# Start-up loads, warm-up, one scaling and the raw weight loads moved in a single-core fp32 transformer block

## The chip, the core and the metric

The kernel runs on one NeuronCore of a Trainium2 chip. The time is the device time in microseconds (us) of one execution; the median of several runs is compared. Engines are named as in the profile: PE (TensorE, matmul), PEld (its weight load), DVE (VectorE), ACT (ScalarE), POOL (GpSimd), SP (SyncE, which here only issues DMAs).

## The reference

One adaLN transformer block: 2048 tokens, width 640, 32 heads of 20, MLP width 1728, all in fp32.

```python
mod = (_silu(c) @ w_mod).reshape(c.shape[0], 6, 1, -1)
sa, ca, ga, sb, cb, gb = (mod[:, 0], mod[:, 1], mod[:, 2], mod[:, 3], mod[:, 4], mod[:, 5])
h = _layernorm(x, axis=-1) * (1 + ca) + sa
x = x + ga * _A_ref(h, A_wqkv, A_w_phi, A_wo)
h = _layernorm(x, axis=-1) * (1 + cb) + sb
x = x + gb * _B_ref(h, B_w1, B_b1, B_w2, B_b2)
```

`_A_ref` is linear attention: q and k are multiplied per head by `w_phi`, turned into features by two softmaxes (of the value and of its negative), and O = phi_q (phi_k^T V) / (phi_q phi_k^T 1), followed by `wo`. `_B_ref` is an MLP whose activation is the square of relu: `r = relu(x @ w1 + b1)`, then `(r * r) @ w2 + b2`.

## The kernel before

**Arithmetic.** Every fp32 operand of a large product is split into a high part and a low part in a reduced format: ACT writes the high part (an activation with Copy, or with the real function), DVE then the low part (`lo`, line 80). A product is the sum of three PE passes, high by high, high by low, low by high (`three` and `mm`, line 70). So each weight tile needs a "hi" on ACT and a "lo" on DVE before PE may use it, and it occupies a slot of the pool `w` (21 slots of 128 x 2 x 640).

**Stages** (times of the profiled execution). The start, to about 60 us: a hand-written order for all five engines (`first`, a manual schedule that begins on line 180). The middle, 60 to 245 us: q, k and v of the other token tiles, laid out by a scheduler. Then the attention numerators, `wo` and the second layer norm, 245 to 350 us. Then the MLP in four groups of 512 tokens (`group(g)`, g = 0 to 3), with a piece of attention between the second and the third. In the groups PE, DVE and ACT follow the code (`by_hand`), SP and POOL are ordered by the scheduler.

**The start in detail.** SP loads, in order: c_t, the transposed conditioning vector (128 x 5, line 183); bd_t, `w_phi` as a block-diagonal matrix (128 x 640, line 185); the raw k weights (`load_raw`, a piece of 40 rows on line 190, five of 128 x 640 on line 192); the first pair of token tiles xb; the raw q weights; the modulation weights wm and so on. Completion semaphores of DMAs are handed out in rotation, eight of them, so the ninth load is issued when the first has landed.

PE begins with `WARM` matmuls on a tile of ones (line 553; each is two passes in the profile, so 28 for 14), then folds: `fold(nm, d)` multiplies one chunk of the raw weight by bd_t (line 241; 12 passes) into two PSUM tiles of the tag `pj`, which has four buffers, so two folds fill it. `split` writes the high parts on ACT (line 248) and the low parts on DVE (line 80), and these free the buffers. ACT's own order in the start is: table load and the exponential ce of c_t (line 222, for silu(c)), neg (line 227), then the splits of the folds. The folds of k come first, then the statistics and scaling of the first tile pair (`stats`, line 486; `scale`, line 502: two activations on line 504), the folds of q, and the modulation vectors cols_a.

Then `k_step(d)`, d = 0 to 4, accumulates chunk d of the k product pk of two token tiles. It needs chunk d of the transposed, modulated input: ACT's hfa (line 338) and hT (line 340) and DVE's low half (line 80), which `out0(d + 1)` issues one step ahead. In that loop the statistics of the second tile pair XB[1] are taken after d = 1 and its scaling issued after d = 2:

```python
        if d == 1:
            n1 = stats(XB[1], "a1")
        if d == 2:
            scale(XB[1], *n1)
```

After the loop ACT makes one high part of the v weights (`v_hi`, line 595) and takes pk out of PSUM (`to_sb`, k on line 391); pq uses the same four buffers next.

**The MLP weights.** 28 pieces (W1 and W2, 14 chunks each, the last one half wide), each loaded raw (rw, line 1065 for W1, 1067 for W2), then split (hi on line 1074, lo on line 80). `prep_load` takes the next slot from a list `places` and loads the raw piece into a row of the pools s1, s2 or s4; `prep_hi` and `prep_lo` fill the slot. Slots are used in rotation, so a new piece takes one that another tile has held, among these XM[j], the residual rows of token tile pair j. `group(0)` issues the loads, splits and lows a few pieces ahead of PE: `p_load(2 * f + 11 - ...)` makes sure that 2f + 11 of the pieces are issued by step f.

**Second layer norm in the groups.** `back(j)` stores the normalised rows of pair j to memory (xn, on ACT's queue, line 1150) and loads them back block by block (sb, four DMAs on SP, line 1161); `turn(j)` transposes them on DVE (fa_q, lines 1171 and 1172). `up` products (matmul with W1) go to ACT for bias and relu (r, line 1375) and for the square (r2t, lines 1384 and 1387), `acc` and `acr` are the products with W2.

## Time and profile before

| what | value |
| --- | --- |
| three runs | 788.79, 790.90, 790.81 us; median 790.81 |
| the profiled execution | 790.26 us |
| its span in the trace | 788.6 us (so 1.66 us lie around the span) |
| PE busy | 777.0 us, 99% of the span |
| DVE, ACT, POOL busy | 553.8, 403.0, 76.5 us |
| DMA | 142.31 MB, mean 180 GB/s |

Rows of the profile give the start and the length in us, the engine, the line, the operation, the tile written and the tiles read, the number of instructions that a row holds, and in brackets how long the engine had been idle and what ended the wait. SPq and ACTq are issues of DMAs. Where a row holds several matmuls, its length is from the first start to the last end, and neighbours overlap a little.

### The profile page before, as it was taken

Reading aid. Unit: us, or ns where it says so; the run is one execution under the profiler, and the core shown is the slowest. Engines: PE = TensorE matmul, PEld = TensorE weight load, DVE = VectorE, ACT = ScalarE, POOL = GpSimd, SP = SyncE. Lnnn points to the kernel's source line nnn. Section 1 sums busy time; section 2 is a strip of 40 time slices with the busy share of each in tenths; the row PEclk is TensorE's granted clock in tenths of the full one; section 3 lists DMA queues with packets and bytes.
Section 4 is the critical chain, followed back from the end, with each engine's and each line's share of the span. In section 5 each row is a group of like instructions: output and inputs, shape, how many; then the busy total and the mean of one; then the engine's idle time right before and its main releaser. Section 6 shows DMA issues by size and latency. Waiting matters only on the chain.

```text
span 788.6 us, 13327 instructions
## 1 busy us (share of the span) xinstructions
PE 777.0 (99%) x5171; PEld 717.4 (91%) x5171; DVE 553.8 (70%) x917; ACT 403.0 (51%) x789; POOL 76.5 (10%) x181
## 2 busy tenths in 40 slices
PE   9999999999999999999989999999999999999997
PEld 8899999999998988898979989999899999989997
DVE  4498999999766488664869699966945343575544
ACT  4667585655734344655938354531265644433221
POOL 3002020000000022201323000100010001000000
PEclk9999999999999999999999999999999999999999
DMA  8713248234121253567798747995779755145121
GB/s 329 265 36 132 101 163 278 90 140 152 54 84 34 84 185 137 167 188 243 245 350 293 249 165 265 282 330 201 206 234 343 274 169 166 51 150 200 34 84 67
DMA packets 76437, 142.31 MB, mean 180 GB/s; under 512 B 12718, under 2 KB 37422, under 8 KB 76374
## 3 DMA queue, kind: packets, MB, share of 16 engines
q1 hardware_dynamic: 69382, 117.74, 45.5%
q0 software_dynamic: 4096, 16.78, 5.6%
q10 hardware_dynamic: 2896, 6.94, 2.3%
q8 instruction: 40, 0.66, 0.3%
q14 instruction: 23, 0.19, 0.1%
HBM read 98.40 MB, written 42.93 MB: 179 GB/s over the span
## 4 chain that ended last, share of the span: by engine, by line
PE 80%; DVE 7%; DMA 5%; ACT 4%; POOL 2%; issue 1%; SPq 0%; ACTq 0%; DVEq 0%; POOLq 0%
PE up L70 20%; PE acc L70 13%; PE pv L70 9%; PE acr L70 8%; PE pk L70 8%; PE pq L70 8%; PE pwo L70 7%; PE kvp L415 3%; DMA xn<-xm 2%; DVE dn L813 2%; DVE scr L811 1%; DMA rw<-in_w 1%; DVE ezb L832 1%; PE ta L325 1%; DMA raw_k<-in_wk 1%
## 5 line engine op out<-in xcount | busy, mean ns | idle before, releaser
L70 PE MATMUL up<-h,w 128*128 128x512 f32 (+1 forms) x910 | 198.3, 371 | 2.9 <-ACT r L1375 2.7
L70 PEld LDWEIGHTS up<-h,w 128*128 128x128 f32 x910 | 155.7, 188 | 31.1 <-ACT r L1375 3.1
L70 PE MATMUL acc<-w,r2t 128*128 128x384 f32 x656 | 151.0, 336 | 0.1
L70 PE MATMUL acr<-w,r2t 128*128 128x256 f32 x656 | 112.8, 279 | 0.0
L70 PEld LDWEIGHTS acc<-w,r2t 128*128 128x128 f32 x656 | 107.5, 188 | 4.6 <-DVE r2t L80 0.4
L70 PEld LDWEIGHTS acr<-w,r2t 128*128 128x128 f32 x656 | 105.6, 188 | 0.0
L70 PE MATMUL pk<-wk,hT 128*128 128x320 f32 x480 | 79.8, 313 | 1.5 <-ACT hT L340 0.9
L70 PE MATMUL pwo<-wo,ot 128*128 128x320 f32 (+1 forms) x512 | 79.5, 313 | 0.1
L70 PE MATMUL pv<-wv,hT 128*128 128x360 f32 (+1 forms) x480 | 77.7, 311 | 0.0
L70 PEld LDWEIGHTS pwo<-wo,ot 128*128 128x128 f32 (+1 forms) x512 | 75.7, 188 | 1.1 <-DVE xm L1043 0.4
L70 PE MATMUL pq<-wq,hT 128*128 128x320 f32 x480 | 76.4, 314 | 0.1
L70 PEld LDWEIGHTS pk<-wk,hT 128*128 128x128 f32 x480 | 71.5, 188 | 3.7 <-ACT hT L340 1.4
L70 PEld LDWEIGHTS pv<-wv,hT 128*128 128x128 f32 x480 | 72.6, 188 | 0.3
L70 PEld LDWEIGHTS pq<-wq,hT 128*128 128x128 f32 x480 | 70.6, 188 | 1.6 <-ACT k L391 0.6
L1375 ACT ACTIVATE r<-up,b_t 128x512 f32<-128x512 f32 x52 | 35.0, 679 | 68.1 <-PE up L70 60.1
L80 DVE TENSOR_TENSOR r2t<-r,r2t 128x512 fp32r<-128x512 f32 (+1 forms) x56 | 38.4, 685 | 34.9 <-ACT r2t L1387 32.1
L80 DVE TENSOR_TENSOR w<-rw,w 128x640 fp32r<-128x640 f32 (+2 forms) x42 | 33.2, 814 | 28.3 <-ACT w L1074 16.9
L1386 DVE TENSOR_TENSOR r<-r 128x512 f32<-128x512 f32 x26 | 17.9, 690 | 47.1 <-ACT r L1375 47.1
L1387 ACT ACTIVATE r2t<-r 128x512 fp32r<-128x512 f32 x52 | 32.9, 633 | 22.4 <-DVE r L1386 21.6
L1477 ACT ACTIVATE w<-rw 128x640 fp32r<-128x640 f32 x42 | 30.6, 730 | 26.3 <-DVE rw L1476 24.1
L338 ACT ACTIVATE hfa<-ta,cols_a 128x256 f32<-128x256 f32 x30 | 17.0, 565 | 28.7 <-PE ta L325 28.6
L1074 ACT ACTIVATE w<-rw 128x640 fp32r<-128x640 f32 x28 | 19.4, 727 | 18.9 <-DMA xn<-xm 10.7
(241 smaller groups left out, 1079.7 us busy)
## 6 DMA issues: line engine op xcount, KB each, us to landing
rw<-in_w SPq DMA_DIRECT2D x65, 320.0 KB, 4.4
w<-w2d SPq DMA_DIRECT2D x28, 320.0 KB, 5.0
w<-w1d SPq DMA_DIRECT2D x12, 640.0 KB, 4.5
esp<-eq SPq DMA_DIRECT2D x11, 640.0 KB, 3.6
wm<-in_w_mod SPq DMA_DIRECT2D x20, 320.0 KB, 3.6
xb<-in_x SPq DMA_DIRECT2D x8, 640.0 KB, 4.1
el<-esp SPq DMA_DIRECT2D x8, 640.0 KB, 4.0
xx<-in_x SPq DMA_DIRECT2D x16, 320.0 KB, 3.5
```

The costliest lines, as they stand in the source:

```text
L70: nc.tensor.matmul(o, a, b, start=first and i == 0, stop=last and i == len(terms) - 1, skip_group_check=skip,)
L80: (eng or nc.vector).tensor_tensor(out_lo, full, hi.bitcast(F32), op=ALU.subtract)
L325: nc.tensor.transpose(p[:, i * P : (i + 1) * P], xn[:, i, d * P : (d + 1) * P], ident)
L338: nc.scalar.activation(hf, p[:, :256], AF.Identity, bias=cols[:, d : d + 1], scale=cols[:, 5 + d : 6 + d])
L415: nc.tensor.matmul(kvp[64 * c : 64 * c + 64, g // 4, a : a + 2 * n].rearrange("p (s n) -> p s n", s=2), v[:, u], e[:, :, o : o + n], start ...
L811: nc.vector.tensor_tensor(z, flat(ET[t]), flat(zb), op=ALU.mult)
L813: nc.vector.tensor_reduce(dn.rearrange("p s h -> p (s h)"), heads(z), axis=AX.X, op=ALU.add)
L1074: nc.scalar.activation(w[:, 0], RAW[k, f], AF.Copy)
L1375: nc.scalar.activation(r, UP[f], AF.Relu, bias=b1_t[:, f : f + 1])
L1386: nc.vector.tensor_tensor(r, r, r, op=ALU.mult)
L1387: nc.scalar.activation(t[:, 0], r, AF.Copy)
L1477: nc.scalar.activation(w[:, 0], raw, AF.Copy)
```

## The change

Four edits in one:

1. bd_t is loaded on ACT's DMA queue, and c_t, first on SP before, is now issued behind the raw k weights. In `load_raw` the piece of 40 rows comes after the first of the five large ones.
2. `WARM` is 10 for 14, so 20 passes for 28.
3. The scaling of the second tile pair is issued after d = 3 for d = 2.
4. `prep_load` no longer takes the slot of the pool `w`; `prep_hi` does. The target of `p_load` is 2f + 15 for 2f + 11.

```diff
-WARM = 14
+WARM = 10
...
-    nc.sync.dma_start(c_t, c)
     bd_t = row("s4", "bd_t")
-    nc.sync.dma_start(bd_t, bd)
+    nc.scalar.dma_start(bd_t, bd)
...
         raw[nm] = [tok2("w", f"raw_{nm}{i}") for i in range(3)]
-        nc.sync.dma_start(raw[nm][2][:40, 1], w1)
         for d in range(NC):
             nc.sync.dma_start(raw[nm][d // 2][:, d % 2], w5[d * P : (d + 1) * P])
+            if d == 0:
+                nc.sync.dma_start(raw[nm][2][:40, 1], w1)
...
     load_raw("k", wk5, wk1)
+    nc.sync.dma_start(c_t, c)
     load_x(0)
...
-        if d == 2:
+        if d == 3:
             scale(XB[1], *n1)
...
-    def prep_load(k, f, w):
+    def prep_load(k, f):
         n = FS[f]
-        W = W1 if k == "1" else W2
-        if k == "1":
-            w = w.rearrange("p s (k n) -> p s k n", k=NC)
-        W[f] = w
...
     def prep_hi(k, f):
-        w = (W1 if k == "1" else W2)[f]
+        w = places.pop(0)(f"w{k}_{f}")
+        if k == "1":
+            w = w.rearrange("p s (k n) -> p s k n", k=NC)
+        (W1 if k == "1" else W2)[f] = w
         nc.scalar.activation(w[:, 0], RAW[k, f], AF.Copy)
...
-                prep_load(k, f, places.pop(0)(f"w{k}_{f}"))
+                prep_load(k, f)
...
-                p_load(2 * f + 11 - (2 * NF - len(todo["load"])))
+                p_load(2 * f + 15 - (2 * NF - len(todo["load"])))
```

The start on SP and ACT. SP's queue at the program's begin, before (raw_k_126 to 128 hold the raw k weights, in_c and in_bd are the inputs of c_t and bd_t):

```order
L183 DMA c_t<-in_c 128x5
L185 DMA bd_t<-in_bd 128x640
L190 DMA raw_k_128<-in_wk 40x640
L192 DMA raw_k_126<-in_wk 128x640 x2
L192 DMA raw_k_127<-in_wk 128x640 x2
L192 DMA raw_k_128<-in_wk 128x640
L196 DMA xb_135<-in_x 128x2x640
```

The same place after the change (raw_k_125 to 127 are the same tiles):

```order
L190 DMA raw_k_125<-in_wk 128x640
L192 DMA raw_k_127<-in_wk 40x640
L190 DMA raw_k_125<-in_wk 128x640
L190 DMA raw_k_126<-in_wk 128x640 x2
L190 DMA raw_k_127<-in_wk 128x640
L206 DMA c_t<-in_c 128x5
L196 DMA xb_135<-in_x 128x2x640
```

On ACT, after the change, the issue of bd_t stands first; ce, which reads c_t, still stands ahead of neg and of the splits:

```order
L184 DMA bd_t<-in_bd 128x640
L223 ACT_TABLE_LOAD
L223 ACTIVATE ce<-c_t 128x5
L228 ACTIVATE neg<-ident 128x128
L249 ACTIVATE wk_281<-foldk_0_282 128x360
```

So c_t moved from the first place of SP's queue to the seventh, and bd_t left that queue, while ACT's compute instructions kept their order.

The first MLP group on SP: the loads that the profile has at 383 to 410 us, before (rw_f of 128x640 is chunk f of W2, of 128x5x128 or 128x5x64 of W1; sb_4521 and sb_4664 are the rows of the pairs 2 and 3 loaded back from xn_211 and xn_212):

```order
L1065 DMA rw_9_4389<-in_w 128x5x128
L1067 DMA rw_9_4627<-in_w 128x640
L1067 DMA rw_7_4470<-in_w 128x640
L1065 DMA rw_11_4563<-in_w 128x5x128
L1067 DMA rw_10_4696<-in_w 128x640
L1067 DMA rw_8_4560<-in_w 128x640
L1067 DMA rw_12_4764<-in_w 128x640
L1161 DMA sb_4521<-xn_211 32x8x160 x4
L1065 DMA rw_13_4699<-in_w 128x5x64 x2
L1065 DMA rw_12_4630<-in_w 128x5x128
L1161 DMA sb_4664<-xn_212 32x8x160 x4
```

The same place after the change (the pairs 2 and 3 are sb_4521 and sb_4665):

```order
L1062 DMA rw_9_4249<-in_w 128x5x128
L1064 DMA rw_9_4471<-in_w 128x640
L1064 DMA rw_10_4561<-in_w 128x640
L1064 DMA rw_8_4387<-in_w 128x640
L1064 DMA rw_12_4631<-in_w 128x640
L1062 DMA rw_13_4563<-in_w 128x5x64 x2
L1062 DMA rw_12_4473<-in_w 128x5x128
L1161 DMA sb_4521<-xn_211 32x8x160 x4
L1161 DMA sb_4665<-xn_212 32x8x160 x4
```

Here W2 chunk 7 and W1 chunk 11 left the place, and the three raw loads of the last chunks went ahead of sb_4521. The two that left now stand at the front of the group's queue, ahead of the sb loads of pair 1 and with the store of x_2:

```order
L1064 DMA rw_4_4216<-in_w 128x640
L1062 DMA rw_8_4222<-in_w 128x5x128
L1064 DMA rw_7_4317<-in_w 128x640
L1062 DMA rw_11_4389<-in_w 128x5x128
L1046 DMA x_2_262<-xm_3756 128x1280
L1161 DMA sb_3949<-xn_210 32x8x160 x4
```

Before, sb of pair 1 followed directly on rw_8, and x_2 on that.

## The prediction

> **What bounds the kernel now.** I read the page's busy shares first, then the table of stages, then PE's list of waits.

> ```profile
> span 788.6 us, 13327 instructions
> PE 777.0 (99%) x5171; PEld 717.4 (91%) x5171; DVE 553.8 (70%) x917; ACT 403.0 (51%) x789; POOL 76.5 (10%) x181
> ```

> TensorE (PE) is busy for 777.0 of 788.6 us. All its idle time is 11.6 us, so no edit that only removes waiting can bring more, and most of that cannot be had: PE starts at 1.06 us, and the last results are stored after it has ended (about 4 us, from the row of 784.40 below). The columns of the next table are the stretch, its length, then each engine's busy time and count.

> ```profile
> 8.10:34.70 26.60, 26.42 (x259) 23.09 (x260) 14.50 (x40) 14.61 (x34) 2.74 (x8) 1.00 0.94 364
> ...
> 60.00:245.00 185.00, 184.07 (x1382) 176.17 (x1382) 162.50 (x215) 116.03 (x255) 16.74 (x30) 1.00 0.38 129
> ```

> Idle PE time: 0.18 us in the start from the second fold on, 0.93 us in the 185 us in the middle. PE's waits name the releasers (total, times, longest):

> ```profile
> PE up L70 <- ACT r L1375: 2.7, 2, 1.9
> ...
> PE pk L70 <- ACT hT L340: 0.9, 1, 0.9
> PE pk L70 <- DVE hT L80: 0.6, 1, 0.6
> ```

> The first two are in places that the change touches (the first MLP group and the start); the third lies in the middle. So I look for gains of 1 to 3 us, and for any new wait in the start, where PE has almost no slack to give.

> **Edits 1 and 2: loads of the start, warm-up.** PE, ACT, the first low half on DVE, and SP's issues:

> ```profile
> 1.06 5.39 PE L553 MATMUL warm<-ones 128*128 128x128 f32 x28 [1.06 <-POOL ones L129]
> 6.28 1.64 PE L241 MATMUL foldk<-bd_t,raw_k 120*128 120x120 f32 x12
> 8.10 6.66 PE L241 MATMUL foldk<-bd_t,raw_k 120*128 120x120 f32 x48 [0.18 <-DMA raw_k<-in_wk]
> ```

> ```profile
> 2.47 0.21 ACT L222 ACTIVATE ce<-c_t 128x5 f32<-128x5 f32 x1 [0.38 <-DMA c_t<-in_c]
> 2.82 0.31 ACT L227 ACTIVATE neg<-ident 128x128 fp32r<-128x128 f32 x1
> 7.17 0.47 ACT L248 ACTIVATE wk<-foldk 128x360 fp32r<-128x360 f32 x1 [4.04 <-PE foldk L241]
> ```

> ```profile
> 7.68 0.53 DVE L80 TENSOR_TENSOR wk<-foldk,wk 128x360 fp32r<-128x360 f32 x1 [4.37 <-ACT wk L248]
> ```

> ```profile
> 0.81 0.39 SPq L183 DMA_DIRECT2D c_t<-in_c  x1
> 1.25 0.42 SPq L185 DMA_DIRECT2D bd_t<-in_bd  x1
> ...
> 10.41 2.04 SPq L200 DMA_DIRECT2D wm<-in_w_ss  x2
> ```

> ```profile
> raw_k<-in_wk SPq DMA_DIRECT2D x5, 320.0 KB, 6.2
> ```

> ```profile
> 1.06:5.27 4.21, 4.21 (x19) 4.21 (x20) 0.53 (x3) 1.54 (x3) 3.90 (x22) 1.00 0.68 187
> ```

> Warm-up: 19 passes take 4.21 us (0.22 us each), the other nine the 1.01 us from 5.27 to 6.28 (0.11 us each): the clock doubled at 5.27. Eight passes of the fast kind go, 8 x 0.11 = 0.9 us; twenty remain, of which the last begins at the doubling. What hides the saving: the second fold waits for its raw rows at 8.10 already, so this is worth at most what the rows come earlier.

> The loads: c_t no longer opens SP's queue, so the large loads start one issue earlier, 1.25 - 0.81 = 0.44 us. But c_t now stands behind all six raw_k pieces, and ACT's first compute instruction reads it. Behind that on ACT stand neg and every split of a fold. A fold's two PSUM tiles come from four buffers, so two folds can be computed before the third needs a buffer that ACT and DVE have emptied. Before, ACT got c_t at 2.44 and could split at once.

> When does c_t land now? The last raw_k piece frees the semaphore for the load issued at 10.41, so it landed at about 10.39; the pieces took 6.2 us each from issue to landing although each is only 320 KB, so they wait for one another in the queue. With the earlier start: 10.39 - 0.44 = 9.95 us, and c_t (2.5 KB) with it. From c_t to a free buffer: neg begins 2.82 - 2.44 = 0.38 later; the split can follow about 0.25 us after neg's start; the low half starts 7.68 - 7.17 = 0.51 after the split and takes 0.53; 0.03 for the semaphore. Sum 1.7 us, so the third fold starts at 9.95 + 1.7 = 11.65. Before, it started at 8.10 + 6.66 / 4 = 9.77. The start gets 11.65 - 9.77 = 1.9 us longer, and as PE then has only 0.18 us of idle time until 34.7, nothing absorbs it: splits, statistics and scaling all hang on the folds and shift along. Bounds: c_t lands with the piece before the last, 0.8 us earlier (320 KB at the 409 GB/s that the queue reaches), or not earlier than 10.39: +1.1 to +2.3. I take 1.9, by the rows of the queue as it is.

> [...] No row of before has two queues loading in the start.

> **Edit 3: second input tile scaled one step later.** ACT, DVE and PE around it:

> ```profile
> 34.95 1.73 ACT L504 ACTIVATE xb<-xb,nba,sqa 128x640 f32<-128x640 f32 x2 [0.60 <-POOL nba L499]
> ...
> 37.17 0.42 ACT L340 ACTIVATE hT<-hfa 128x256 fp32r<-128x256 f32 x1
> 37.49 0.72 ACT L595 ACTIVATE wv<-rawv 128x640 fp32r<-128x640 f32 x1
> 38.55 1.75 ACT L391 ACTIVATE k<-pk 128x320 f32<-128x320 f32 x4 [0.34 <-PE pk L70]
> ```

> ```profile
> 35.00 0.16 DVE L530 TENSOR_REDUCE cols_a<-kvp 128x2 f32<-128x4 f32 x1 [0.45 <-PE kvp L529]
> 37.61 0.43 DVE L80 TENSOR_TENSOR hT<-hfa,hT 128x256 fp32r<-128x256 f32 x1 [2.45 <-ACT hT L340]
> ```

> ```profile
> 37.63 2.19 PE L70 MATMUL pk<-wk,hT 128*128 128x320 f32 x12 [0.91 <-ACT hT L340]
> 39.66 1.63 PE L70 MATMUL pq<-wq,hT 128*128 128x320 f32 x10
> ```

> (Times of before; the shift of 1.9 us applies to all.) The scaling holds ACT until 36.6 while hfa could begin when DVE's reduction ends, 35.16. With it behind, hfa and hT take 35.2 to 36.2, the low half ends at 36.65, and PE's wait of 0.91 from 36.72 on goes; pk ends 0.91 earlier. Next late is ACT: scaling (1.73, to about 37.9), wv's high half (0.72), then the first k out of PSUM at about 38.45 instead of 38.55, done at 38.95. The pq products need its buffer: they start at about 39.0 for 39.66. Gain 0.65 us, between 0.3 (if ACT comes late by as much as its own gaps here, 0.34) and 0.91 (if the buffer is free in time).

> **Edit 4: raw MLP weights loaded before a slot is free.** The larger of the two waits of `up`:

> ```profile
> 407.81 1.36 ACT L1074 ACTIVATE w<-rw 128x640 fp32r<-128x640 f32 x2 [10.67 <-DMA xn<-xm]
> ```

> ```profile
> 409.80 3.72 PE L70 MATMUL up<-h,w 128*128 128x512 f32 x15 [1.88 <-ACT r L1375]
> ```

> ```profile
> 397.16 0.42 ACTq L1150 DMA_DIRECT2D xn<-xm  x1
> ```

> ```profile
> 392.86 2.66 SPq L1161 DMA_DIRECT2D sb<-xn  x4
> 397.25 7.11 SPq L1065 DMA_DIRECT2D rw<-in_w  x3
> ```

> ```profile
> 397.00:408.00 11.00, 10.92 (x66) 10.02 (x64) 5.11 (x8) 0.33 (x2) 2.16 (x5) 1.00 1.08 361
> ```

> The name of what ACT waits for is the point: not the raw rows, but the store of xn, which reads the tile whose slot the split weights are to take. The edit moves the raw load, which was not late here; the split still takes that slot and still waits for that store. What the edit does change is the traffic. The store was issued at 397.16 and landed at 407.78 (10.6 us) with all DMA engines busy, behind four loads of sb issued just before, and beside three raw loads that SP took 7.11 us to issue. In the new order the raw loads stand ahead of those four sb loads, and W2 chunk 7 and W1 chunk 11 stand 14 rows earlier in SP's queue. So the store meets less. It is early enough if it lands 1.9 us sooner, by 405.9. I take the 1.88 us as gone, less 0.4 for what is late next (an estimate: half of the smaller wait of `up`, 2.7 - 1.9 = 0.8): gain 1.5 us. Bounds: the whole stall, 1.9, and a loss of 0.8, if the loads put ahead make the smaller wait as long again. That smaller wait stays otherwise, since its raw load uses the same slot at the same time.

> On the other side the four sb loads come later: issued from 397.25 + 7.11 = 404.4 to 406.9 for 392.86 to 395.5. DVE turns them here:

> ```profile
> 413.83 2.23 DVE L1171 STREAM_TRANSPOSE fa_q<-sb 128x256 f32<-128x256 f32 x4
> ```

> With the stall gone that is about 412, so 5 us remain for a load that took 3.4 us in quieter traffic (row below). I cost it at nothing; if the cover fails, each us that sb comes late can cost PE one.

> **The middle.** The scheduler lays out 60 to 245 us in a slightly other order; PE idles 0.93 us there. I take 0, bounds -0.5 and +0.5.

> **Sum.** Against the profiled execution of 790.26 us (span 788.6, 1.66 around it; the median of the three runs, 790.81, is 0.55 above it): +1.9 - 0.65 - 1.5 + 0 = -0.25, that is 790.0 us. Its own range: 788.0, with all four terms at their good bounds (-0.8 - 0.26 - 0.4 - 0.5), to 792.0, with start, scaling and middle at their bad ones and half of the stall left (0.4 + 0.35 + 0.5 + 0.75). A measurement of this kernel tells about 0.3% (2.4 us) from no change: faster is below 787.9, slower above 792.6.

> **The rivals.**

> *c_t is not held up by the queue.* Its 2.5 KB might pass the large pieces. Then two folds run as rows arrive, 0.44 us earlier, and the warm-up is short enough for it: -0.44 - 0.65 - 1.5 = -2.6, 787.7 us, faster. Against it: the 6.2 us of raw_k above, which is queueing. Chance 0.12.

> *The store is as late as before.* Then edit 4 does nothing for the time, which is the case in which the change doesn't do what it says: 791.5 us. For it: the same slot, the same store, the DMA engines full (1.08). Chance 0.20.

> *sb late in the first half-group: slower.* SP's queue before and DVE:

> ```profile
> 341.82 2.51 SPq L1161 DMA_DIRECT2D sb<-xn  x4
> ```

> ```profile
> 350.11 2.27 DVE L1171 STREAM_TRANSPOSE fa_q<-sb 128x256 f32<-128x256 f32 x4
> ```

> ```profile
> sb<-xn SPq DMA_DIRECT2D x4, 160.0 KB, 3.4
> ```

> ```profile
> 342.00:350.00 8.00, 8.00 (x57) 7.78 (x56) 5.21 (x13) 4.33 (x10) 0.00 (x0) 1.00 0.66 200
> ```

> Two raw loads (320 KB each) and the 640 KB store of x now stand ahead of these sb loads. The last of them is issued at about 343.7 and lands 3.4 later, 347.1; the transposes follow at 350.1, so the slack is 3.0 us. At the 409 GB/s of the start 1.3 MB take 3.2 us; at the 200 GB/s of this stretch 6.5 us, and the transposes are 3.5 us late, which PE, 8.00 of 8.00 busy here, then waits for: 793.5 us. It decides from a delay of 3.0 us on. Against: the DMA share is only 0.66, so part of the 1.3 MB fits into gaps. Chance 0.15.

> *The clock falls back.* PE is now idle from about 9.3 to 11.65. A drop shows at the end:

> ```profile
> 784.40:786.90 2.50, 0.05 (x1) 0.00 (x0) 0.74 (x2) 0.00 (x0) 0.00 (x0) 1.00 0.66 262
> 786.90:788.60 1.70, 0.00 (x0) 0.00 (x0) 0.00 (x0) 0.00 (x0) 0.00 (x0) 0.51 0.01 5
> ```

> There 2.5 us without work passed at full clock, and only then it halved. If 2.35 us suffice here, PE runs at half speed for the 4.2 us that the first warm-up took and loses 2.1: 792.1 us. Chance 0.08. [...]

> **How the numbers follow.** Forecast 0.45 (790.0), and the rivals 0.12, 0.20, 0.15, 0.08. Faster: 0.12, and 0.05 of the forecast, whose low end lies at the limit: 0.17. Slower: all of the late sb, and 0.02 of the clock with a store that stays late: 0.17. The rest, 0.66, is no difference that can be told. The range goes from 787.2, below the passing c_t, to 793.5, the late sb at its full price.

> **What would show it.** Right: ACT's first compute instruction starts at about 10 us and PE has a hole of about 2 us ahead of the third fold; no wait ahead of the last pk; ACT's wait for xn ending about 2 us earlier, relative to PE's own place, and no 1.88 at `up`. Wrong: c_t landing before 6 us; the third fold starting at or before 9.8; the wait at `up` unchanged; DVE's transposes near 350 waiting for sb; PE's fold passes 0.22 us apart after the hole.

## The result and the profile after

The changed kernel takes 799.01 us (median of six runs, 795.9 to 802.6) against 790.72 us before: ratio 1.0113, 95% interval 1.0085 to 1.0141. It is 1.1% slower. The profiled execution took 798.65 us, its span is 796.9 us.

The page of the changed kernel points at the cause in its row of clocks (PEclk, in tenths of full speed, for 40 slices of 19.9 us each):

```profile
span 796.9 us, 13312 instructions
...
PEclk7699999999999999999999999999999999999999
```

Before, every digit was 9. Now TensorE's clock is low in the first two slices. PE and ACT in the start, and PE's waits in the whole execution (total, times, longest):

```profile
1.06 3.95 PE L554 MATMUL warm<-ones 128*128 128x128 f32 x20 [1.06 <-POOL ones L129]
5.10 3.36 PE L242 MATMUL foldk<-bd_t,raw_k 120*128 120x120 f32 x24
12.02 9.05 PE L242 MATMUL foldk<-bd_t,raw_k 120*128 120x120 f32 x36 [3.56 <-DVE wk L80]
```

```profile
10.50 0.21 ACT L223 ACTIVATE ce<-c_t 128x5 f32<-128x5 f32 x1 [7.98 <-DMA c_t<-in_c]
10.61 0.29 ACT L228 ACTIVATE neg<-ident 128x128 fp32r<-128x128 f32 x1
10.93 1.43 ACT L249 ACTIVATE wk<-foldk 128x360 fp32r<-128x360 f32 x4
```

```profile
PE foldk L242 <- DVE wk L80: 3.6, 1, 3.6
...
PE up L70 <- ACT r L1375: 0.9, 1, 0.9
PE pq L70 <- ACT k L392: 0.4, 1, 0.4
```

ACT stands for 7.98 us behind the wait for c_t. The splits follow at once when it has landed, four in a row: they had been due. PE did two folds by 8.46 us, then stood idle for 3.56. After that, 36 passes (three folds) take 9.05 us, where 48 (four folds) took 6.66 before: 0.25 us for one pass against 0.14. The table of stretches shows why; the number behind POOL's count is the clock granted to PE:

```profile
4.13:7.54 3.41, 3.32 (x27) 2.97 (x26) 0.00 (x0) 0.00 (x0) 1.77 (x9) 1.00 1.03 351
7.54:10.96 3.42, 0.92 (x8) 0.69 (x6) 0.18 (x2) 0.43 (x3) 0.00 (x0) 1.00 1.00 353
10.96:34.85 23.89, 22.83 (x108) 20.42 (x108) 9.74 (x24) 8.98 (x20) 1.40 (x4) 0.50 0.73 293
34.85:45.00 10.15, 10.15 (x129) 8.57 (x129) 5.26 (x16) 4.88 (x12) 0.00 (x0) 1.00 0.32 98
```

The clock halves at 10.96 us, inside the hole, and stays at half for 23.9 us, although PE works without a pause from 12.02 on.

The same matmul in the two traces tells where the time goes. The third fold starts at 12.02 for 9.75: 2.3 us later. The first pk, before and after:

```profile
27.14 2.03 PE L70 MATMUL pk<-wk,hT 128*128 128x320 f32 x12
```

```profile
39.22 2.02 PE L70 MATMUL pk<-wk,hT 128*128 128x320 f32 x12
```

It is 12.1 us late, so between the two matmuls another 9.8 us were lost, and PE had no idle time there: this is work at half the clock. From there on the changed kernel wins time back: the first pq is 11.25 us late, the first `up` 11.35 (361.20 for 349.85), the last matmul of the first MLP group 8.96, the last matmul of all 8.67, and the span is 8.3 longer. So the place of the scaling brought 0.8, the first group 2.4, the end 0.3 and a little at the store; the middle cost 0.1.

The scaling, on ACT and PE:

```profile
48.19 1.72 ACT L505 ACTIVATE xb<-xb,nba,sqa 128x640 f32<-128x640 f32 x2
49.82 0.72 ACT L596 ACTIVATE wv<-rawv 128x640 fp32r<-128x640 f32 x1
50.45 1.39 ACT L392 ACTIVATE k<-pk 128x320 f32<-128x320 f32 x4
```

```profile
46.79 3.77 PE L70 MATMUL pk<-wk,hT 128*128 128x320 f32 x24
50.91 4.66 PE L70 MATMUL pq<-wq,hT 128*128 128x320 f32 x30 [0.35 <-ACT k L392]
```

All 24 pk matmuls run in one piece, without the 0.91 us; 0.35 of it comes back as pq's wait for ACT, as laid out in the prediction. In the first MLP group:

```profile
414.64 1.37 ACT L1074 ACTIVATE w<-rw 128x640 fp32r<-128x640 f32 x2 [6.19 <-DMA xn<-xm]
```

```profile
419.25 3.60 PE L70 MATMUL up<-h,w 128*128 128x512 f32 x15
```

ACT still waits for the store of xn, but 6.19 us in place of 10.67, and the store itself takes about 6.1 us from issue to landing for 10.6:

```profile
408.48 0.37 ACTq L1150 DMA_DIRECT2D xn<-xm  x1
```

So `up` has no idle time ahead of it any more. The other wait of `up`, 0.9 in the list above, stayed.

### The profile page after: what moved, and what is told of

The parts are those of the page before. It is cut to its first block, busy times and chain, and to the rows that moved or that the text cites. A ratio compares the mean times of both kernels' runs of the same rounds, so it can differ in the third digit from the quotient of the medians.

```text
span 796.9 us, 13312 instructions
## 1 busy us (share of the span) xinstructions
PE 785.1 (99%) x5163; PEld 725.0 (91%) x5163; DVE 553.4 (69%) x917; ACT 402.2 (50%) x789; POOL 80.4 (10%) x181
## 4 chain that ended last, share of the span: by engine, by line
PE 85%; DVE 5%; DMA 4%; ACT 2%; POOL 1%; issue 1%; SPq 1%; DVEq 0%; ACTq 0%; POOLq 0%
PE up L70 22%; PE acc L70 14%; PE acr L70 9%; PE pv L70 9%; PE pk L70 9%; PE pq L70 8%; PE pwo L70 5%; PE kvp L416 3%; PE foldq L242 2%; DMA xn<-xm 2%; DVE dn L814 2%; DVE scr L812 1%; PE foldk L242 1%; DMA rw<-in_w 1%; PE ta L326 1%
## 5 line engine op out<-in xcount | busy, mean ns | idle before, releaser
L70 PE MATMUL up<-h,w 128*128 128x512 f32 (+1 forms) x910 | 198.0, 371 | 1.1 <-ACT r L1375 0.9
L70 PEld LDWEIGHTS up<-h,w 128*128 128x128 f32 x910 | 155.7, 188 | 28.9 <-ACT r L1375 1.1
L70 PE MATMUL acc<-w,r2t 128*128 128x384 f32 x656 | 150.7, 336 | 0.0
L70 PE MATMUL acr<-w,r2t 128*128 128x256 f32 x656 | 112.8, 279 | 0.0
L70 PEld LDWEIGHTS acc<-w,r2t 128*128 128x128 f32 x656 | 107.5, 188 | 4.2 <-DVE w L80 0.2
L70 PEld LDWEIGHTS acr<-w,r2t 128*128 128x128 f32 x656 | 105.6, 188 | 0.0
L70 PE MATMUL pwo<-wo,ot 128*128 128x320 f32 (+1 forms) x512 | 79.5, 313 | 0.1
L70 PE MATMUL pk<-wk,hT 128*128 128x320 f32 x480 | 79.0, 313 | 0.1
L70 PE MATMUL pv<-wv,hT 128*128 128x360 f32 (+1 forms) x480 | 78.3, 312 | 0.0
L70 PE MATMUL pq<-wq,hT 128*128 128x320 f32 x480 | 76.7, 314 | 0.5 <-ACT k L392 0.4
L70 PEld LDWEIGHTS pwo<-wo,ot 128*128 128x128 f32 (+1 forms) x512 | 75.8, 188 | 1.1 <-DVE xm L1044 0.4
L70 PEld LDWEIGHTS pk<-wk,hT 128*128 128x128 f32 x480 | 71.5, 188 | 2.5 <-issue 0.9
L70 PEld LDWEIGHTS pv<-wv,hT 128*128 128x128 f32 x480 | 72.4, 188 | 0.4
L70 PEld LDWEIGHTS pq<-wq,hT 128*128 128x128 f32 x480 | 70.6, 188 | 2.1 <-ACT k L392 1.3
L1375 ACT ACTIVATE r<-up,b_t 128x512 f32<-128x512 f32 x52 | 35.0, 680 | 67.9 <-PE up L70 59.9
L80 DVE TENSOR_TENSOR r2t<-r,r2t 128x512 fp32r<-128x512 f32 (+1 forms) x56 | 38.4, 685 | 33.1 <-ACT r2t L1387 30.4
L80 DVE TENSOR_TENSOR w<-rw,w 128x640 fp32r<-128x640 f32 (+2 forms) x42 | 33.3, 814 | 23.8 <-ACT w L1074 12.4
L1074 ACT ACTIVATE w<-rw 128x640 fp32r<-128x640 f32 x28 | 19.4, 727 | 17.3 <-DMA rw<-in_w 8.4
```

Of the source, the lines that this page charges most:

```text
L70: nc.tensor.matmul(o, a, b, start=first and i == 0, stop=last and i == len(terms) - 1, skip_group_check=skip,)
L80: (eng or nc.vector).tensor_tensor(out_lo, full, hi.bitcast(F32), op=ALU.subtract)
L1074: nc.scalar.activation(w[:, 0], RAW[k, f], AF.Copy)
L1375: nc.scalar.activation(r, UP[f], AF.Relu, bias=b1_t[:, f : f + 1])
```

## The experiments

Two theories. **Clock:** the late c_t holds ACT; PE falls idle; the clock halves and does not come back while PE does folds. **Warm-up:** ten matmuls for 14 are too few to keep the clock. A third, that the lateness of c_t costs the time by itself, without the clock, was tried beside them.

**c_t first again.**

```diff
+    nc.sync.dma_start(c_t, c)
     bd_t = row("s4", "bd_t")
     nc.scalar.dma_start(bd_t, bd)
...
     load_raw("k", wk5, wk1)
-    nc.sync.dma_start(c_t, c)
```

> The changed kernel with one thing undone: c_t is loaded first on SP again. Theory (the late c_t holds ACT, PE falls idle for 3.56 us, the clock halves): no idle of PE in the folds, full clock from 4 to 5.5 us on, the first pk 0 to 1.2 us earlier than in the kernel before, and with the 0.8 us of the moved scaling and the 2.4 us of the first MLP group that the changed kernel won back: 786 to 788 us. Rival (ten warm-up matmuls for 14 are too few to hold the clock): the clock still halves within the folds, 796 us or more.

Measured: 786.69 us, ratio 0.9942 to the kernel before (0.9927 to 0.9957), clock full. PE and ACT of this kernel:

```profile
4.96 8.23 PE L242 MATMUL foldk<-bd_t,raw_k 120*128 120x120 f32 x60
```

```profile
3.55 0.21 ACT L223 ACTIVATE ce<-c_t 128x5 f32<-128x5 f32 x1 [1.03 <-DMA c_t<-in_c]
```

Five folds in one piece with the ten warm-up matmuls. So ten warm-up matmuls are enough as long as PE does not stand idle behind them, and the warm-up theory falls. The place of one load of 2.5 KB makes the difference between 0.6% faster and 1.1% slower.

**The readers of c_t behind the splits.** c_t stays late; ce, the steps on DVE that follow it, and neg are issued behind the third fold's split.

```diff
-    nc.scalar.activation(ce, c_t, AF.Exp, scale=-1.0)
...
     for d in range(3):
         fold("k", d)()
+    nc.scalar.activation(ce, c_t, AF.Exp, scale=-1.0)
...
```

> The changed kernel with ce, cs and neg, the readers of c_t, issued on ACT and DVE behind the splits of the third fold. c_t is as late as in the changed kernel. Theory (ACT standing in order behind the wait for c_t is what costs): no idle of PE in the folds, no fall, 786 to 788 us, like c_t loaded first. Rival (c_t itself is needed early, or the order of the loads costs): 797 us or more.

Measured: 786.19 us, ratio 0.9937 (0.9924 to 0.9949): the lowest median of all, though not told apart from c_t first. ACT's first split here:

```profile
6.91 0.47 ACT L242 ACTIVATE wk<-foldk 128x360 fp32r<-128x360 f32 x1 [4.38 <-PE foldk L235]
```

It waits for the fold, not for a load. c_t landed at 9.1 us here, long after that split, and its first reader, at 11.3, found it there. So c_t may come late; what must not be is a wait for it ahead of the splits on ACT.

**The hole filled.** The wait stays, and PE gets work for it.

```diff
     for d in range(3):
+        if d == 2:
+            for i in range(15):
+                nc.tensor.matmul(warm[:, :P], ones, ones, start=True, stop=True)
         fold("k", d)()
```

> The changed kernel with 15 more matmuls on ones (30 passes, about 3.4 us at full clock) on PE between the second and the third fold, where it was idle. c_t is as late as in the changed kernel. Theory: the third fold starts at about 12.0 as before, but the clock does not fall, and the 9.8 us between the third fold and the first pk come back: 788.5 to 790 us. Rival (the lateness of c_t costs the time by itself, through ACT and DVE): 797 to 799 us.

Measured: 789.58 us, ratio 0.9981 (0.9972 to 0.9990). PE and the clock around the fill:

```profile
8.89 3.62 PE L558 MATMUL warm<-ones 128*128 128x128 f32 x30
12.35 4.91 PE L242 MATMUL foldk<-bd_t,raw_k 120*128 120x120 f32 x36
```

```profile
9.34:12.75 3.41, 3.41 (x33) 3.41 (x32) 2.21 (x7) 1.67 (x6) 0.00 (x0) 1.00 1.04 410
12.75:40.00 27.25, 27.05 (x264) 23.88 (x264) 13.56 (x38) 15.78 (x35) 2.98 (x8) 1.00 0.76 287
```

The third fold starts even later, at 12.35, yet its 36 passes take 4.91 us for 9.05, and 9.4 us are back. Useless work on PE made the kernel 1.2% faster than the idle hole; this shows the clock as the larger part of the cost. The delay is the smaller part, and it is paid at full clock too: the first pk is 2.5 us later than before, and 3.75 later than with c_t first (25.90), which was 2.9 us faster than this kernel.

```profile
29.65 2.03 PE L70 MATMUL pk<-wk,hT 128*128 128x320 f32 x12
```

**Only c_t late, and only the warm-up put back.** The first is the kernel before with c_t behind the raw k weights, the second the changed kernel with `WARM = 14`.

```diff
-    nc.sync.dma_start(c_t, c)
...
     load_raw("k", wk5, wk1)
+    nc.sync.dma_start(c_t, c)
```

> The kernel before with one thing done: c_t is loaded behind the raw k weights. Warm-up, bd_t and everything else as before. Theory: c_t lands at about 10.5 us, the third fold starts at about 12.1, PE is idle for about 2.4 us from 9.7 on; if this idle time is enough for the clock to halve, 801 to 803 us, if it is too short, 793 us. Rival (the short warm-up is the cause): no fall, 793 us.

> The changed kernel with 14 warm-up matmuls. The two folds then end at about 9.3 us and PE is idle for about 2.7 us. Theory: an idle time of that length still halves the clock (2.5 us without work stood ahead of the fall at the end of the kernel before), 797 to 800 us. Rival (the warm-up was too short): 788.5 to 791 us.

Both split in two. c_t alone: 790.73 us once, at full clock, and 804.9 to 805.9 three times, at a mean clock of 0.980 to 0.982. With 14 warm-up matmuls: 787.4 to 788.3 four times at 0.999 or 1.000, and 796.1 to 803.9 six times at 0.979 to 0.989. The profiled one of each had the fall; c_t alone:

```profile
7.54:10.95 3.41, 1.86 (x14) 1.58 (x13) 0.88 (x4) 1.26 (x5) 0.00 (x0) 1.00 1.04 387
10.95:41.67 30.72, 30.48 (x168) 26.74 (x168) 11.59 (x29) 11.61 (x26) 1.41 (x4) 0.50 0.57 227
```

With 14 matmuls:

```profile
8.77:12.18 3.41, 2.16 (x18) 1.81 (x16) 2.22 (x7) 2.22 (x7) 0.00 (x0) 1.00 1.01 390
12.18:39.49 27.31, 27.31 (x149) 23.92 (x152) 10.25 (x25) 9.98 (x23) 1.41 (x4) 0.50 0.60 240
```

Neither expectation fits as a whole. The holes were 1.79 and 1.25 us, shorter than I had worked out (ACT read c_t at 9.67 and 9.31 in these), and still the clock fell; in some of the other executions it did not. In these profiles and that of the changed kernel the changes of the clock in the start lie a whole number of 3.41 us apart: 6.83 (2), 23.89 (7), 27.31 (8), 30.72 (9). At full clock the kernel before ran from 5.28 to 786.93 us and the changed kernel from 34.85 to 796.02: 781.65 and 761.17 us, 229 and 223 times a ninth of the 30.72. I read this as a clock that changed only where such a stretch of 3.41 us ended. Whether it falls would then depend on how a hole of this size lies in the stretches; that only some executions had the fall for this reason was not shown. The stretches that tipped had PE busy for 0.92 (changed kernel), 1.86 (c_t alone) and 2.16 (14 matmuls) of 3.41 us, with folds. The runs without the fall have no profile, so it is not known how long their hole was; the one of c_t alone, 790.73 us, lies within the runs of the kernel before (790.0 to 792.6 beside it).

**The first group and the scaling alone.** The kernel before with edit 4, and with edit 3.

```diff
-            if d == 2:
+            if d == 3:
                 scale(XB[1], *n1)
```

> The kernel before with one thing done: raw MLP weights loaded ahead of their slots (2f + 15). Theory by the traces: the 1.88 us wait of up and about 0.5 us beside it go: 2.4 us in the first MLP group, 788 to 788.7 us, 0.3% faster. Rival (the gain in the changed kernel came from another phase of the transfers): no difference.

> The kernel before with one thing done: the scaling of the second tile pair after d = 3. Theory by the traces: 0.8 us at the first pq, kept to the end: 789.5 to 790.2 us, about 0.1% faster. Rival (ACT gives it back later): no difference.

Edit 4: 788.71 us, ratio 0.9969 (0.9956 to 0.9981), 0.3% faster; its waits of `up` are down to the one of 0.9. ACT's wait for the store, which was 10.67:

```profile
405.24 1.37 ACT L1073 ACTIVATE w<-rw 128x640 fp32r<-128x640 f32 x2 [7.51 <-DMA xn<-xm]
```

Edit 3: 790.18 us, ratio 0.9988 (0.9977 to 1.0000), as expected in size, with an interval that just reaches no difference.

**Passes behind the third fold.** Can dense work bring the clock back? In the changed kernel with 16 more matmuls on ones behind the third fold:

```diff
     for d in range(3):
         fold("k", d)()
+    for i in range(16):
+        nc.tensor.matmul(warm[:, :P], ones, ones, start=True, stop=True)
```

> The changed kernel with 16 matmuls on ones (32 passes) on PE after the third fold, at about 15 us, when the clock is at half. Theory (a window of 3.4 us that is filled without a break raises the clock; the folds, with their breaks, do not): the clock is full by 18 to 21.5 us instead of 34.85; the 32 passes cost 5 to 6.8 us, about 9 of the 9.8 us are partly saved: 795 to 798 us. Rival (the clock comes back a fixed time after the fall): full only at about 35 us, and the passes are added: 803 to 806 us.

Measured: 794.48 us (792.8 to 795.5). The time lies a little below the range expected, but the profiled execution has no fall in the start to repair: its hole was 1.19 us, from 9.26 to 10.45, and lay across the end of a stretch. The stretch with the first part of it reads

```profile
6.54:9.95 3.41, 2.71 (x20) 2.32 (x19) 0.62 (x4) 1.00 (x4) 0.00 (x0) 1.00 1.04 395
```

It kept the clock with 2.71 us of work. So the passes had nothing to raise here, and the time must be lost elsewhere. The trace shows where most of it goes: in the first MLP group ACT waits for raw weights, PE stands for 2.30 us ahead of `up`, for 0.80 in the kernel with the hole filled, and the clock falls there, for one stretch:

```profile
375.18:378.59 3.41, 1.11 (x6) 0.79 (x5) 0.83 (x1) 2.22 (x4) 0.55 (x1) 1.00 0.61 197
378.59:382.00 3.41, 3.41 (x10) 2.63 (x9) 1.64 (x3) 3.41 (x8) 0.22 (x1) 0.50 0.36 102
```

The clock is full again after one stretch that `up` fills without a pause, where the work of the start needed seven to nine. For the start the question stays open with this run. I therefore made the hole long in every execution, by moving c_t behind the first xb too, once without the passes and once with them.

```diff
-    nc.sync.dma_start(c_t, c)
     load_x(0)
+    nc.sync.dma_start(c_t, c)
```

> The changed kernel with c_t one place further back on SP, behind the first xb (640 KB), so that c_t lands at about 12 us and PE is idle for some 4 to 5 us ahead of the third fold in every execution. Theory: the clock falls in every execution, about 1.6 us are added to the changed kernel: 799 to 805 us.

> As the kernel with c_t behind the first xb, with 16 matmuls on ones (32 passes) on PE behind the third fold. Theory (a stretch of 3.4 us without breaks raises the clock, the folds with their breaks do not): full clock 3.4 to 8 us after the third fold starts, 3 to 6 us faster than without the passes. Rival (the clock comes back a fixed time, some 24 us, after the fall): the clock rises as late as without them, and the 32 passes at half clock add 6.8 us.

Measured: 800.70 us without (797.9 to 803.0) and 797.18 with (796.9 to 797.5). The holes were 4.36 and 4.71 us. The stretches and the first pk without:

```profile
7.47:10.88 3.41, 0.68 (x6) 0.45 (x4) 0.00 (x0) 0.00 (x0) 0.00 (x0) 1.00 0.93 356
10.88:34.78 23.90, 22.28 (x106) 20.08 (x106) 9.93 (x25) 9.42 (x22) 1.41 (x4) 0.50 0.72 291
```

```profile
39.49 2.02 PE L70 MATMUL pk<-wk,hT 128*128 128x320 f32 x12
```

and with the passes, then the passes themselves and the first pk:

```profile
8.20:11.62 3.42, 0.22 (x2) 0.10 (x1) 0.00 (x0) 0.01 (x1) 0.00 (x0) 1.00 1.00 377
11.62:21.86 10.24, 8.73 (x39) 8.44 (x40) 5.15 (x15) 2.70 (x8) 1.40 (x4) 0.50 1.03 413
21.86:30.00 8.14, 8.14 (x64) 7.50 (x64) 3.74 (x8) 4.79 (x10) 0.00 (x0) 1.00 0.77 306
```

```profile
16.13 6.56 PE L558 MATMUL warm<-ones 128*128 128x128 f32 x32
37.66 2.02 PE L70 MATMUL pk<-wk,hT 128*128 128x320 f32 x12
```

The clock is back after 10.24 us (three stretches) for 23.90 (seven), at the end of the first stretch that the passes fill wholly (18.44 to 21.86). The first pk comes 1.8 us earlier, although 6.56 us of useless work stand ahead of it. The medians are 3.5 us apart, and not all of that comes of the start: the profiled execution without the passes has, as the one above, a fall in the first MLP group, from 386.35 to 389.76, behind a wait of `up` of 1.99 us, and the one with them has a wait of 0.84 there and no fall. So the range of 799 to 805 us expected without the passes was met in part by luck: its first pk is only 0.27 us later than that of the changed kernel. What the clock did in the start is plain even so: 10.24 and 23.90 us are not one fixed time, and with the folds alone it came back no sooner than after seven stretches.

**The warm-up by itself.** c_t first, with 14 warm-up matmuls.

> The changed kernel with c_t first on SP again and 14 warm-up matmuls. Theory A (the raw rows come early enough that the folds follow the warm-up directly): eight passes at full clock, 0.9 us, slower than with ten: 787 to 788 us. Theory B (as in the prediction: the second fold waits for its rows anyway): as with ten, 786.2 to 787.

Measured: 787.79 us, ratio 0.9963 (0.9950 to 0.9977), against 786.69 and 0.9942 (0.9927 to 0.9957) with ten. The intervals overlap, and the profiled execution, the fastest of its five, took 786.69 as well, so the time does not decide. The profile shows theory A at work, the folds start at 6.72 for 4.96, right behind the warm-up:

```profile
1.06 5.83 PE L554 MATMUL warm<-ones 128*128 128x128 f32 x28 [1.06 <-POOL ones L129]
6.72 8.20 PE L242 MATMUL foldk<-bd_t,raw_k 120*128 120x120 f32 x60
```

With c_t first and ten matmuls the first pk starts at 25.90 for 27.14 before, so the rest of edit 1 together with edit 2 is worth about 1.2 us, if c_t is not in the way.

## Why the prediction was wrong

**The step that failed** is the rival "the clock falls back". It named the mechanism, gave it a chance of 0.08 and a price of 2.1 us, and put it at nothing in the sum; it came in every run of the changed kernel (mean clock 0.981 to 0.987), and cost 9.8 us in the profiled one. One of the prediction's own signs of being wrong, fold passes some 0.22 us apart behind the hole, turned up (0.25). Three things were wrong in it.

*The hole.* I worked it out as 2.35 us, from 9.3 to 11.65. It was 3.56, from 8.46 to 12.02. The end was late by 0.37, since c_t landed at 10.48 instead of 9.95, outside even my later bound of 10.39. The start was 0.8 us early, as the warm-up ended sooner, the clock rose at 4.13 for 5.28 (this moment differs from profile to profile: 5.36 in that with 14 warm-up matmuls), and the raw rows of the second fold were there by 6.74 for 8.10. I had let the edits meet in the third fold's start alone and had not asked what they do to the hole between.

*The rule for a fall.* I took the end of the kernel before, where 2.5 us without work went by at full clock, as a sign that such a hole is too short. But that fall came 229 of the stretches of 3.41 us after the rise, and the last of them, 783.52 to 786.93, still had 0.93 us of work in it: by my reading the 2.5 us showed where a stretch ended, not how long a hole must be. A hole of 1.25 us among folds was enough in the profiled run with 14 warm-up matmuls. Nor was the stretch ahead of a fall idle: in the trace of the changed kernel it had 0.92 us of work in it, and in that with 14 warm-up matmuls 2.16 of 3.41.

*The way back.* I priced the low clock at 4.2 us, the length of the first warm-up, at half speed. It lasted 23.9 us. The folds, the transposes and the modulation products of the start did not raise it before the end of the seventh stretch; behind the passes on ones it rose at the end of the first stretch that they filled (18.44 to 21.86), and with `up` in the first MLP group after one (378.59 to 382.00). This is the big error: 9.8 us for 2.1.

**The other terms.** The start without the clock: 2.3 us for 1.9, within its bounds of 1.1 to 2.3, by the mechanism named (ACT in order behind c_t, four buffers for two folds). Scaling: 0.83 for 0.65, right, with the wait of pq named ahead. First MLP group: 2.4 for 1.5, above the bound of 1.9; the store comes early enough, and that the order of the loads does it is argued, not tried by itself. What I had put as late next, 0.4, did not come, and about 0.5 us more went in small waits that were not followed one by one. But the smaller wait of `up`, which I had taken to stay, moves with the arrival of raw weights: with edit 4 it was 0.73 to 2.30 us in the profiled executions. Middle: 0.1 lost for 0. Had the clock held, the terms would have made about 789.6 (2.3 - 0.8 - 2.4 + 0.1 - 0.3 on 790.7), and the filled hole, which kept the clock and the delay, gave 789.6.

**The other rivals.** c_t past the queue: no, it landed at 10.48. The store as late as before: no. The late sb: no; the loads came about 2.3 us later against PE than before (issued from 355.52 on for 341.82, while `up` was 11.35 late), within the 3.0 of slack, and the transposes of pair 1 still ran right behind DVE's work, with no wait:

```profile
360.74 0.82 DVE L80 TENSOR_TENSOR w<-rw,w 128x640 fp32r<-128x640 f32 x1 [0.79 <-ACT w L1074]
361.48 2.29 DVE L1171 STREAM_TRANSPOSE fa_q<-sb 128x256 f32<-128x256 f32 x4
```

The four sb loads of the other place, which I had costed at nothing, did make DVE wait 4.02 us (its transposes start at 424.77 for 413.83), but PE had no wait there.

On the queues of the start: bd_t and the first piece of raw_k, both issued at 0.80 us, on two queues, landed within 0.3 us of each other, at 5.05 and 4.8. The first fold started as bd_t was there, at 5.10. The small load behind the last piece landed no earlier than the last piece did before, 10.48 for 10.39, so the 0.44 us of the earlier start did not show there.

## What to carry to other kernels

A load moved back in a queue is priced at its readers, and at everything in order behind the first reader on that engine, however small the load is: here 2.5 KB held ACT for 7.98 us. Where such a wait opens a hole on TensorE, the price need not be the hole alone: ask whether the clock falls in it, and how soon the work behind it raises it again. Here the delay cost 2.3 us and the low clock 9.8. If a hole can't be closed at once, try filling it with matmuls whose result nobody reads: 15 of them brought 9.4 us back here. A kernel whose times spread over several us is worth a look at where the granted clock falls in its trace: here it did so in the start, and in two profiled executions in the first MLP group.

## What the runs showed of the hardware

```profile
408.05:411.46 3.41, 1.66 (x7) 1.40 (x8) 2.88 (x4) 2.96 (x5) 1.08 (x2) 1.00 0.82 221
```

Nor did the length of a hole: in the profile of c_t alone late, PE stood for 2.28 us ahead of `up` across the end of a stretch, which left 2.35 and 2.19 us of work in the two, and the clock stayed full, while 1.99 us lost it, with c_t behind xb, where they left 1.42 in one. What does decide it stays open, and so does why the rise came with the seventh stretch of the changed kernel and not with the sixth, where PE was as busy (3.41 of 3.41 us in both). The landing of the same small load behind the same raw pieces moved between 8.9 us (passes behind the third fold) and 10.5 (the changed kernel) from one profiled execution to another.
